# Turning the gated keys and queries in a recurrent attention plus FFN kernel: copies in destination order for the first chunk, DMA transposes for the later units

## The chip, the core and the metric

The kernel runs on one core of one Trainium2 chip. TensorE (PE in the profile; PEld is its weight load), VectorE (DVE), ScalarE (ACT), GpSimd (POOL) and SyncE (SP) each run their own instruction stream in order and meet through semaphores. Transfers are issued from SP's, ACT's or POOL's stream and run on 16 DMA engines. The metric is the time of one execution on the device, in microseconds; of several runs the median is taken.

## The reference

Inputs `q`, `k`, `v`, `f_logit` have the shape (4, 8, 768, 48): batch, heads, steps, head dimension. Per batch and head a 48 x 48 state is carried over 768 steps, and the result goes through a two-layer FFN:

```
f = 1 / (1 + exp(-f_logit))
for t in range(S):
    state = f[t][:, None] * state + outer(k[t], v[t])
    y[t] = q[t] @ state
x = y, heads side by side, as (B * S, 384)
out = leaky_relu(x @ w_in, 0.01) @ w_out        # 384 -> 2048 -> 384
```

## The kernel before

Steps are cut into six chunks of 128. One chunk of one batch, with all eight heads, is a *unit*: 24 units, numbered chunk by chunk, four batches to a chunk. Inside a unit the recurrence becomes matmuls. With L the running sum of -log f, keys are multiplied by exp(L) (`em_t`) and queries by exp(-L) (`a_t`); these scaled tiles `kh`, `qh` have the steps on the partitions and the eight heads, padded from 48 to 64, along the free dimension. They are then turned, so that head dimensions lie on the partitions, two heads to a block of 128: `kT`, `qT`. Scores are `kT` against `qT` (`score_pe`, 8 matmuls), masked to the upper triangle (`mask_dve`), multiplied with v, and the state's part is added (`mix_pe`). `state_pe`, `state_dve`, `state_pool` carry the state on. The result is copied (`y_out`), transposed (`x_pe`, `x_out`) and goes into the FFN, where two units form one row block of 256: `up` (6 matmuls of 256 columns per bank), `up_act` (leaky ReLU on ACT), `down` (8 matmuls of 384 columns, called twice per unit), `put` (copy on DVE and an output store issued on SP). The first row blocks use the narrower `up_one`, `down_cols` and `put_cols`.

Turning a unit (`turn_pe`, line 325) is eight PE transposes into one PSUM bank, then two DVE copies out of it (`turn_k`, `turn_q`, line 328).

The first chunk (units 0 to 3) is done four batches at once in a *quad* layout: partition 4t+b holds four neighbouring steps 4t to 4t+3 (index j) of batch b. It is computed in two halves of four heads (`hh`). `q_exp_act`, `q_ln_act` make the log gates, `q_gate_pe` their running sum, `q_decay_act` the two exponentials, `q_k_scale`, `q_q_scale` the scaled tiles, `q_turn_pe` their transposes. A transposed tile has in its free dimension the order j, t, b. `q_k_out`, `q_q_out` copy it out of PSUM into `kTq`, `qTq`, which are ordered b, t, j. Line 216 and its neighbours give that copy the order of the source: both sides are walked as j, t, b, so that neighbouring writes lie 256 bytes apart. The lines seen in the profile for these copies are those of the helper `move` (L138 on ACT, L140 on DVE), which also serves `cast_v`, `y_out`, `x_out` and `q_back_out`. `q_score_pe`, `q_mask`, `q_mask_pool`, `q_mix_pe` then do for the quad what the unit functions do later. `idle_pe` issues matmuls on zeros whose result nobody reads (L132).

The order of everything is written out by hand: 868 calls, one after the other, each with its PSUM bank numbers. Every engine runs its part of the list in that order. `load_part` calls (f, k, q, v of a unit; 192 KB each, on SP, in rings of six buffers) and the stores of `put` stand in the same list, so SP's stream is a fixed interleaving of loads and stores; a store waits on SP for DVE's copy, and what stands behind it waits too. At most eight transfers issued from SP and ACT are outstanding: each waits for the landing of the eighth before it.

The FFN weights are cast and loaded by POOL (`load_w_in`, `load_w_out`).

Of the kernel before, what the change touches and what calls it, by code (L numbers as in the profile page):

```python
# [9 lines left out]
FP32 = mybir.dt.float32  # L10
# [6 lines left out]
def kernel(  # L17
# [45 lines left out]
    fq = [const.tile([128, 4, 4, D], FP32, name=f"fq{i}", tag=f"fq{i}") for i in range(2)]  # L63
    kq = const.tile([128, H, 4, D], FP32, tag="kq")
    qq = [const.tile([128, 4, 4, D], FP32, name=f"qq{i}", tag=f"qq{i}") for i in range(2)]

    def load_quad(eng, t, src, b, lo, n):
        eng.dma_start(out=t[b::4, :, :, :].rearrange("p h j d -> p h (j d)"),
                      in_=src[b, lo:lo + n, 0:C, :].rearrange("h (t j) d -> t h (j d)", j=4))

    for hh in range(2):
        for b in (2, 3):
            load_quad(nc.scalar, fq[hh], f_logit, b, 4 * hh, 4)
    for hh in range(2):
        for b in (0, 1):
            load_quad(nc.sync, fq[hh], f_logit, b, 4 * hh, 4)
    for b in range(B):
        load_quad(nc.sync, kq, k, b, 0, H)
    for hh in range(2):
        for b in range(B):  # L80
            load_quad(nc.sync, qq[hh], q, b, 4 * hh, 4)

    nc.scalar.preload_act_table_set("natural_log_exp_and_others")
# [27 lines left out]
    qhs = [const.tile([128, H, 64], BF16, name=f"qh{i}", tag=f"qh{i}") for i in range(3)]  # L111
    khs = [const.tile([128, H, 64], BF16, name=f"kh{i}", tag=f"kh{i}") for i in range(4)]
# [12 lines left out]
    for t in lfs + khs + qhs:  # L125
        nc.vector.memset(t[:, :, D:64], 0.0)
    for t in state_b:
        nc.vector.memset(t, 0.0)
# [19 lines left out]
    turned = {name: ring(name, 3, [128, P2, 128], BF16) for name in ("kT", "qT")}  # L148
# [36 lines left out]
    def q_exp_act(hh):  # L185
        nc.scalar.activation(fq[hh], fq[hh], AF.Exp, scale=-1.0)

    def q_ln_act(hh):
        nc.scalar.activation(lfq[hh][:, :, :, 0:D], fq[hh].rearrange("p h j d -> p j h d"), AF.Ln, bias=1.0)
# [18 lines left out]
    def q_q_scale(eng, hh, a):  # L208
        q_scale_half(eng, qhq, qq[hh], aq, hh, a)
# [104 lines left out]
    def q_scale(u):  # L314
        r = raw[u]
        nc.gpsimd.tensor_mul(qhs[u % 3][:, :, 0:D], r["q"], a_ts[u % 3])  # L316
# [4 lines left out]
    def turn_pe(u, bk):  # L321
        tp = bank16(bk).rearrange("p (i a n) -> p i a n", i=2, a=P2)
        for i, src in enumerate((khs[u % 4], qhs[u % 3])):
            for p in range(P2):
                nc.tensor.transpose(tp[:, i, p, :], src[:, 2 * p:2 * p + 2, :], ident)  # L325

# [112 lines left out]
    idle_pe(31, 7)  # L439
# [8 lines left out]
    q_end_pe(2)  # L448
    q_gate_pe(1, 0, 3)
    q_decay_act(0, 0, emq, 1.0, 0)  # L450
    q_k_scale(V, 0, 1)
    q_end_act(2)
    q_k_scale(V, 0, 0)
    q_gate_pe(1, 1, 4)
    q_decay_act(0, 0, aq, -1.0, 0)
    q_decay_act(0, 1, aq, -1.0, 1)
    q_q_scale(V, 0, 0)
    q_turn_pe(khq, 0, 0, 5)
    q_turn_pe(khq, 0, 1, 5)
    q_decay_act(1, 1, emq, 1.0, 4)  # L460
    q_q_scale(G, 0, 1)
    q_turn_pe(qhq, 0, 0, 6)
    q_k_out(V, 0, 0, 5)
    idle_pe(4, 7)
    q_decay_act(1, 1, aq, -1.0, 4)
    q_decay_act(1, 0, emq, 1.0, 3)
    q_k_scale(G, 1, 1)
    q_k_out(V, 0, 1, 5)
    q_turn_pe(qhq, 0, 1, 6)
    idle_pe(7, 7)  # L470
    q_decay_act(1, 0, aq, -1.0, 3)
    q_k_scale(V, 1, 0)
    q_q_out(A, 0, 0, 6)
    q_q_scale(G, 1, 0)
    cast_v(V, 0)
    q_turn_pe(khq, 1, 0, 7)
    q_q_out(A, 0, 1, 6)
    q_turn_pe(khq, 1, 1, 7)
    q_q_scale(V, 1, 1)
    load_w_in(0)  # L480
    q_turn_pe(qhq, 1, 0, 2)
    q_k_out(V, 1, 0, 7)
    q_score_pe(0, 1, 0, 1)
    load_w_in(1)
    q_turn_pe(qhq, 1, 1, 2)
    q_wf_act(0, 1, 0, 0)
    q_k_out(V, 1, 1, 7)
    q_score_pe(0, 0, 4, 5)
    cast_v(G, 1)
    idle_pe(2, 6)  # L490
    q_q_out(A, 1, 0, 2)
    cast_v(G, 2)
    q_mask(0, 1, 1, 1)
    q_back_pe(3, 3)
    idle_pe(6, 7)
    q_mask_pool(0, 1, 0)
    q_q_out(A, 1, 1, 2)
    q_mask(0, 0, 1, 5)
    q_score_pe(1, 0, 6, 0)
    q_mask(0, 0, 0, 4)  # L500
    idle_pe(3, 7)
    load_w_in(2)
    q_mask(1, 0, 0, 6)
    q_score_pe(1, 1, 7, 1)
    load_w_in(3)
    idle_pe(7, 5)
    q_wf_act(1, 1, 1, 1)
    load_w_out(0)
    q_mask(1, 0, 1, 0)
    q_wf_act(1, 1, 0, 7)  # L510
    q_back_out(V, 3, 3)
    q_mix_pe(0, 2)
    q_mask_pool(1, 1, 1)
    q_mix_pe(1, 5)
    q_back_pe(0, 4)
    y_out(A, 0, 2)
    y_out(V, 1, 5)
    idle_pe(2, 7)
    q_back_out(A, 0, 4)
    x_pe(0, 6)  # L520
    x_pe(1, 1)
    q_mask_pool(1, 1, 0)
    q_back_pe(2, 0)
    x_out(A, 0, 6)
    x_out(V, 1, 1)
    state_pe(0, 3)
    q_back_out(V, 2, 0)
    up(0, 0, 7)
    q_state_dve(0)
    cast_v(G, 3)  # L530
    q_mix_pe(2, 2)
    up(0, 1, 5)
    up_act(0, 0, 7)
    y_out(V, 2, 2)
    q_state_pool(0)
    up(0, 5, 4)
    up_act(0, 1, 5)
    x_pe(2, 1)
    up(0, 4, 6)
    up_act(0, 5, 4)  # L540
    x_out(V, 2, 1)
    q_mix_pe(3, 0)
    load_part(4, "f", f_logit)
    state_pe(3, 3)
    up_act(0, 4, 6)
    up(0, 7, 7)
    y_out(V, 3, 0)
    q_state_dve(3)
    up(0, 6, 2)
    load_part(4, "k", k)  # L550
    up_act(0, 7, 7)
    x_pe(3, 5)
    q_state_pool(3)
    up(0, 2, 1)
    up_act(0, 6, 2)
    load_part(4, "q", q)
    x_out(A, 3, 5)
    state_pe(2, 4)
    q_back_pe(1, 6)
    q_state_dve(2)  # L560
    up(0, 3, 0)
    up_act(0, 2, 1)
    load_part(4, "v", v)
    up(1, 0, 3)
    q_back_out(V, 1, 6)
    q_state_pool(2)
    up_act(0, 3, 0)
    state_pe(1, 7)
    up(1, 7, 2)
    up_act(1, 0, 3)  # L570
    q_state_dve(1)
    up(1, 4, 5)
    up_act(1, 7, 2)
    q_state_pool(1)
    down_cols(0, 0, 1)
    up_act(1, 4, 5)
    gate_exp(4)
    up(1, 2, 4)
    gate_ln(4)
    put_cols(0, 0, 1)  # L580
    up(1, 1, 6)
    up_act(1, 2, 4)
    gate_pe(4, 0)
    up_act(1, 1, 6)
    up(1, 6, 3)
    decay_em(4, 0)
    load_w_out(1)
    up(1, 5, 7)
    decay_a(4, 0)
    down_cols(1, 0, 2)  # L590
    k_scale(4)
    up_act(1, 5, 7)
    up_act(1, 6, 3)
    load_part(5, "f", f_logit)
    q_scale(4)
    up(1, 3, 5)
    put_cols(1, 0, 2)
    cast_v(G, 4)
    turn_pe(4, 1)
    load_part(5, "k", k)  # L600
    up_act(1, 3, 5)
    state_pe(4, 4)
    turn_k(4, 1)
    down_cols(3, 0, 6)
    load_part(5, "q", q)
    state_dve(4)
    turn_q(4, 1)
    down_cols(2, 0, 0)
    load_part(5, "v", v)
    put_cols(3, 0, 6)  # L610
    load_part(6, "f", f_logit)
    score_pe(4, 7, 3)
    put_cols(2, 0, 0)
    down_cols(3, 1, 2)
    mask_dve(4, 1, 3)
    load_part(6, "k", k)
    mask_dve(4, 0, 7)
    gate_exp(5)
    down_cols(0, 1, 5)
    load_part(6, "q", q)  # L620
    put_cols(3, 1, 2)
    gate_ln(5)
    load_part(6, "v", v)
    mix_pe(4, 4)
    put_cols(0, 1, 5)
    gate_pe(5, 1)
    state_pool(4)
    y_out(A, 4, 4)
    down_cols(2, 1, 6)
    load_part(7, "f", f_logit)  # L630
    decay_em(5, 1)
    decay_a(5, 1)
    k_scale(5)
    load_part(7, "k", k)
    x_pe(4, 0)
    down_cols(1, 1, 3)
    put_cols(2, 1, 6)
    x_out(V, 4, 0)
    gate_exp(6)
    q_scale(5)  # L640
    load_part(7, "q", q)
    gate_ln(6)
    up_one(4, 3, 7)
    cast_v(G, 5)
    put_cols(1, 1, 3)
    load_part(7, "v", v)
    turn_pe(5, 2)
    up_one_act(4, 3, 7)
    up_one(4, 1, 5)
    turn_k(5, 2)  # L650
    load_part(8, "f", f_logit)
    turn_q(5, 2)
    up_one(4, 0, 4)
    up_one_act(4, 1, 5)
    cast_v(G, 6)
    gate_pe(6, 1)
    load_part(8, "k", k)
    up_one_act(4, 0, 4)
    score_pe(5, 6, 0)
    up_one(4, 2, 3)  # L660
    decay_em(6, 1)
    mask_dve(5, 0, 6)
    load_part(8, "q", q)
    gate_exp(7)
    k_scale(6)
    down(4, 0, 7)
    mask_dve(5, 1, 0)
    gate_ln(7)
    load_part(8, "v", v)
    up_one_act(4, 2, 3)  # L670
    mix_pe(5, 2)
    decay_a(6, 1)
    state_pe(6, 5)
    gate_pe(7, 4)
    load_part(9, "f", f_logit)
    state_dve(6)
    down(4, 1, 7)
    y_out(A, 5, 2)
    q_scale(6)
    decay_em(7, 4)  # L680
    load_part(9, "k", k)
    decay_a(7, 4)
    cast_v(G, 7)
    x_pe(5, 6)
    turn_pe(6, 0)
    put(4, 7)
    k_scale(7)
    gate_exp(8)
    state_pe(5, 3)
    load_part(9, "q", q)  # L690
    x_out(V, 5, 6)
    gate_ln(8)
    turn_k(6, 0)
    up_one(5, 3, 1)
    q_scale(7)
    state_dve(5)
    load_part(9, "v", v)
    up_one(5, 1, 2)
    up_one_act(5, 3, 1)
    turn_q(6, 0)  # L700
# [636 lines left out]
```

## Time and profile before

| | |
|---|---|
| median of three runs | 203.26 us (203.01 to 205.38) |
| profiled execution, own time | 203.25 us |
| its span in the profile | 201.5 us |
| PE busy | 186.6 us (93%) |
| DVE, ACT, POOL busy | 96.5, 120.6, 82.1 us |
| first `up` matmul (L402) starts | 31.22 us |
| turning transposes (L325) | 160 matmuls |
| copies of turned units (L328) | 40, mean 423 and 416 ns |
| quad copies (L138, L140, 128x512 bf16 of kTq, qTq) | 8, mean 2532 ns on DVE, 2622 ns on ACT (the second of a pair overlaps the first's start) |
| a load of 192 KB, issue to landing | 3.9 us (median) |

The span is from the first to the last instruction; the execution's own time adds what lies around it, 1.75 us here. Busy times of PE are from modelled ends: its matmuls overlap, so that a group's pitch (time from one start to the next) is what it costs in a full stream, and this is shorter than the mean duration shown. In the timeline, a line gives start, duration, engine, source line, operation, output and inputs, count, and in brackets the idle time ahead of it with what ended it.

### The profile page before, as it was taken

The page shows a single profiled execution, that of the slowest core. Times are in us where ns is not written, and L with a number is a line of the kernel's source. Part 1 is how long each engine was busy: PE and PEld are TensorE (multiplying, and loading weights), DVE is VectorE, ACT ScalarE, POOL GpSimd, SP SyncE. Part 2 cuts the span into 40 slices and gives each one's busy share as a digit, 9 for nine tenths or more (in the row PEclk, how much of TensorE's full clock was granted, in tenths as well). Part 3 has the DMA queues.
Part 4 walks back from the last instruction along what each step waited for, and adds up shares of the span by engine and source line. Part 5 has one row for each costly group of instructions (what it writes and reads, how often), then busy time and mean ns, then how long its engine had stood idle before and what let it go on. Part 6 is the DMA issues. An engine that isn't in the chain of part 4 may idle for free.

```text
span 201.5 us, 5284 instructions
## 1 busy us (share of the span) xinstructions
PE 186.6 (93%) x2094; PEld 146.6 (73%) x2094; DVE 96.5 (48%) x215; ACT 120.6 (60%) x237; POOL 82.1 (41%) x144
## 2 busy tenths in 40 slices
PE   4993599999999979999999999999999999999991
PEld 3782368999997748787778767877878877776660
DVE  6069955405445836954656456333555460111221
ACT  2678935883456768768778666766656734343200
POOL 4046742442444768795467581671632000000000
PEclk9998559999999999999999999999999999999998
DMA  4878999099988999999999899722100011111121
GB/s 130 239 179 129 221 195 164 0 89 226 199 195 183 233 190 235 185 217 188 219 192 235 174 229 204 160 47 74 42 0 3 0 42 39 39 39 42 41 108 50
DMA packets 100537, 27.08 MB, mean 134 GB/s; under 512 B 92320, under 2 KB 100512, under 8 KB 100512
## 3 DMA queue, kind: packets, MB, share of 16 engines
q1 hardware_dynamic: 94208, 23.21, 52.5%
q0 software_dynamic: 5728, 3.15, 11.8%
q10 hardware_dynamic: 576, 0.39, 0.8%
q8 instruction: 16, 0.26, 0.5%
q14 instruction: 9, 0.07, 0.1%
HBM read 25.17 MB, written 4.72 MB: 148 GB/s over the span
## 4 chain that ended last, share of the span: by engine, by line
PE 78%; DVE 6%; DMA 6%; POOL 3%; issue 3%; SPq 2%; ACT 1%; POOLq 0%; DVEq 0%; ACTq 0%
PE ps L402 29%; PE ps L416 23%; PE ps L132 5%; DVE kTq L140 4%; PE ps L325 4%; PE ps L427 3%; PE ps L341 3%; DMA v_raw<-in_v_dram 2%; DMA k_raw<-in_k_dram 2%; DMA f_raw<-in_f_logit_dram 2%; PE ps L385 2%; PE ps L354 2%; PE ps L351 1%; PE ps L362 1%; PE ps L194 1%
## 5 line engine op out<-in xcount | busy, mean ns | idle before, releaser
L411 ACT ACTIVATE gT<-ps 128x512 bf16<-128x512 f32 x88 | 52.1, 597 | 33.8 <-PE ps L402 31.7
L402 PE MATMUL ps<-xT,w_in_b 128*128 128x256 bf16 x528 | 67.8, 273 | 0.2 <-DVE xT L140 0.2
L416 PE MATMUL ps<-w_out_b,gT 128*128 128x384 bf16 x320 | 56.9, 326 | 0.0
L402 PEld LDWEIGHTS <-w_in_b 128*128 128x128 bf16 x528 | 49.1, 98 | 8.0 <-issue 0.3
L416 PEld LDWEIGHTS <-gT 128*128 128x128 bf16 x320 | 30.3, 98 | 17.2
L344 DVE TENSOR_TENSOR wm<-ps,ut 128x512 bf16<-128x512 f32 x40 | 25.9, 686 | 11.1 <-PE ps L341 9.4
L422 DVE COPY osb<-ps 128x384 f32<-128x384 f32 x20 | 11.1, 557 | 37.1 <-PE ps L416 37.1
L312 POOL TENSOR_TENSOR kh<-k_raw,em_t 128x384 bf16<-128x384 f32 x20 | 18.1, 913 | 12.1 <-ACT em_t L304 5.2
L281 POOL CAST sb<-sf 64x192 bf16<-64x192 f32 x40 | 13.6, 341 | 22.8 <-PE ps L351 14.8
L316 POOL TENSOR_TENSOR qh<-q_raw,a_t 128x384 bf16<-128x384 f32 x20 | 18.1, 911 | 4.7 <-ACT a_end L309 1.4
L140 POOL CAST v_b<-v_raw 128x384 bf16<-128x384 f32 x23 | 11.8, 512 | 13.9 <-DMA v_raw<-in_v_dram 10.2
L328 DVE COPY kT<-ps 128x512 bf16<-128x512 bf16 x20 | 8.5, 423 | 16.3 <-PE ps L325 12.7
L288 ACT ACTIVATE f_raw<-f_raw 128x384 f32<-128x384 f32 x20 | 10.5, 526 | 9.4 <-DMA f_raw<-in_f_logit_dram 9.4
L138 ACT CAST xn<-ps 128x384 bf16<-128x384 f32 x21 | 10.0, 480 | 9.6 <-PE ps L354 8.6
L132 PE MATMUL ps<-fill 128*128 128x256 bf16 x65 | 13.4, 373 | 1.1 <-DVE ind L124 1.1
L140 DVE COPY xT<-ps 128x384 bf16<-128x384 bf16 x22 | 7.7, 352 | 8.7 <-PE ps L385 4.7
L427 PE MATMUL ps<-w_out_b,gT 128*128 128x192 bf16 x128 | 11.5, 246 | 0.0
L132 PEld LDWEIGHTS <-fill 128*128 128x128 bf16 x65 | 8.0, 129 | 4.4 <-issue 1.9
L304 ACT ACTIVATE em_t<-ps 128x384 bf16<-128x384 f32 x20 | 9.9, 495 | 2.1 <-PE ps L300 1.4
L291 ACT ACTIVATE lf<-f_raw 128x384 bf16<-128x384 f32 x20 | 10.5, 524 | 0.5
L427 PEld LDWEIGHTS <-gT 128*128 128x128 bf16 x128 | 10.5, 98 | 0.1
L307 ACT ACTIVATE a_t<-ps 128x384 bf16<-128x384 f32 x20 | 9.8, 495 | 0.0
(92 smaller groups left out, 240.5 us busy)
## 6 DMA issues: line engine op xcount, KB each, us to landing
v_raw<-in_v_dram SPq DMA_DIRECT2D x24, 192.0 KB, 3.9
f_raw<-in_f_logit_dram SPq DMA_DIRECT2D x20, 192.0 KB, 3.9
k_raw<-in_k_dram SPq DMA_DIRECT2D x20, 192.0 KB, 4.0
q_raw<-in_q_dram SPq DMA_DIRECT2D x20, 192.0 KB, 3.9
out_dram<-osb SPq DMA_DIRECT2D x20, 192.0 KB, 1.9
w_in_b<-in_moe_w_in_dram POOLq DMA_DIRECT2D x4, 384.0 KB, 7.2
w_out_b<-in_moe_w_out_dram POOLq DMA_DIRECT2D x2, 768.0 KB, 11.3
kq<-in_k_dram SPq DMA_DIRECT2D x4, 192.0 KB, 3.8
```

What stands on the lines that cost most here:

```text
L132: nc.tensor.matmul(bank(bk)[:, 0:256], fill[:, 0:128], fill[:, 0:256], start=True, stop=True)
L140: eng.tensor_copy(out=out, in_=in_)
L281: nc.gpsimd.tensor_copy(out=state_b[b][r, :, e * D:(e + 1) * D], in_=state_f[b][r])
L288: nc.scalar.activation(raw[u]["f"], raw[u]["f"], AF.Exp, scale=-1.0)
L312: nc.gpsimd.tensor_mul(khs[u % 4][:, :, 0:D], raw[u]["k"], em_ts[u % 3])
L316: nc.gpsimd.tensor_mul(qhs[u % 3][:, :, 0:D], r["q"], a_ts[u % 3])
L344: nc.vector.tensor_mul(wms[e][u % 3], bank(bk).rearrange("p (i n) -> p i n", i=P2), ut[:, None, :].to_broadcast([128, P2, 128]))
L402: nc.tensor.matmul(bank(bk)[:, i * 256:(i + 1) * 256], w_in_b[:, kk, ff * 128:(ff + 1) * 128], xTs[m % 3][:, kk].rearrange("p a n -> p (a ...
L411: nc.scalar.activation(gTs[m % GBUFS][:, 2 * g:2 * g + 2].rearrange("p f a n -> p (f a n)"), bank(bk), AF.Prelu, alpha=0.01)
L416: nc.tensor.matmul(bank(bk)[:, 0:KD], gTs[u // 2 % GBUFS][:, ff, u % 2, :], w_out_b[:, ff, :], start=(ff == 0), stop=(ff == NF - 1))
L422: nc.vector.tensor_copy(out=osb, in_=bank(bk)[:, 0:KD])
L427: nc.tensor.matmul(bank(bk)[:, 0:CH], gTs[u // 2 % GBUFS][:, ff, u % 2, :], w_out_b[:, ff, half * CH:(half + 1) * CH], start=(ff == 0), st ...
```

## The change

Three things are different, and the call list is written anew around them.

- **First loads.** f and q of the quad are one tile each, with all heads, in place of two halves: four loads each, not eight. Two of the four k loads go from SP to ACT, behind the table load.
- **Quad copies in destination order.** `q_turn_out` walks both sides as b, t, j. The writes are then contiguous, and the reads from PSUM are 256 bytes apart. The eight copies are also distributed anew: six on ACT, two on DVE (before, four and four).
- **Units 10 to 23** are turned by `turn_dma`, one DMA transpose on SP from the scaled tiles to the turned ones (128 x 1024 bf16, 256 KB). `turn_pe`, `turn_k`, `turn_q` remain for units 4 to 9. For this `kh` and `qh` of a unit become the halves of one tile `kqh`, in a ring of four (`qh` had three), and `kT`, `qT` the halves of one tile `kqT`, in a ring of three.

In the new list the fill matmuls ahead of the first gate go from 31 to 40, most of the first chunk's mixing stands ahead of the first `up`, and unit 5's four loads stand ahead of the first output store (before, behind it). From unit 10 on, loads stand behind each `turn_dma` in SP's stream. The counts of all FFN calls are as before.

```diff
-    fq = [const.tile([128, 4, 4, D], FP32, name=f"fq{i}", tag=f"fq{i}") for i in range(2)]
+    fq = const.tile([128, H, 4, D], FP32, tag="fq")
...
-    for hh in range(2):
-        for b in (2, 3):
-            load_quad(nc.scalar, fq[hh], f_logit, b, 4 * hh, 4)
...
+    for b in (2, 3):
+        load_quad(nc.scalar, fq, f_logit, b)
+    nc.scalar.preload_act_table_set("natural_log_exp_and_others")
+    for b in (2, 3):
+        load_quad(nc.scalar, kq, k, b)
+    for t, src in ((fq, f_logit), (kq, k)):
+        for b in (0, 1):
+            load_quad(nc.sync, t, src, b)
+    for b in range(B):
+        load_quad(nc.sync, qq, q, b)
...
+    kqs = ring("kqh", 4, [128, 2, H, 64], BF16)
+    khs, qhs = [t[:, 0] for t in kqs], [t[:, 1] for t in kqs]
...
+    kqTs = ring("kqT", 3, [128, 2, P2, 128], BF16)
+    turned = {"kT": [t[:, 0] for t in kqTs], "qT": [t[:, 1] for t in kqTs]}
...
     def q_turn_out(dst, hh, bk, pp):
-        tp = bank16(bk).rearrange("p (a j t b) -> p a j t b", a=2, j=4, b=4)
-        o = dst[hh].rearrange("p a b (t j) -> p a j t b", j=4)
-        return dict(out=o[:, pp], in_=tp[:, pp])
+        tp = bank16(bk).rearrange("p (a j t b) -> p a b t j", a=2, j=4, b=4)
+        return dict(out=dst[hh][:, pp].rearrange("p b (t j) -> p b t j", j=4), in_=tp[:, pp])
...
+    def turn_dma(u):
+        nc.sync.dma_start_transpose(out=kqTs[u % 3].rearrange("p i a n -> p (i a) n"),
+                                    in_=kqs[u % 4].rearrange("p i h d -> p (i h d)"))
...
-    idle_pe(31, 7)
+    idle_pe(40, 7)
...
-    turn_pe(15, 1)
...
-    turn_k(15, 1)
...
-    turn_q(15, 1)
-    score_pe(15, 5, 3)
...
+    q_scale(15)
...
+    turn_dma(15)
+    score_pe(14, 2, 6)
...
+    score_pe(15, 5, 3)
```

More of the change, by code (lines that the diff above doesn't have):

```diff
@@ L734 @@
[L734 to L741 removed]
+    load_part(7, "v", v)
+    score_pe(5, 5, 0)
+    put_cols(1, 1, 1)
+    down_cols(3, 1, 3)
+    mask_dve(5, 1, 0)
+    load_part(8, "f", f_logit)
+    mask_dve(5, 0, 5)
+    gate_pe(6, 4)
+    x_pe(4, 2)
+    put_cols(3, 1, 3)
+    load_part(8, "k", k)
+    mix_pe(5, 6)
+    decay_em(6, 4)
+    x_out(V, 4, 2)
+    state_pe(5, 7)
+    decay_a(6, 4)
@@ new lines @@
+    gate_pe(8, 5)
+    state_pool(6)
+    turn_pe(7, 6)
+    load_part(10, "k", k)
+    decay_em(8, 5)
+    down(5, 0, 1)
+    turn_k(7, 6)
+    decay_a(8, 5)
+    turn_q(7, 6)
+    k_scale(8)
+    y_out(A, 6, 7)
+    score_pe(7, 0, 3)
+    load_part(10, "q", q)
+    x_pe(6, 4)
+    cast_v(G, 8)
+    up_one(5, 3, 5)
+    mask_dve(7, 1, 3)
+    q_scale(8)
+    gate_exp(9)
+    state_pe(8, 6)
+    mask_dve(7, 0, 0)
+    up_one(4, 3, 7)
+    up_one_act(5, 3, 5)
+    load_part(10, "v", v)
+    state_dve(8)
@@ new lines @@
+    up(6, 4, 5)
+    load_part(19, "f", f_logit)
+    score_pe(16, 7, 4)
+    up_act(6, 4, 5)
+    mix_pe(15, 0)
+    mask_dve(16, 0, 7)
+    gate_pe(17, 1)
+    state_pool(15)
+    y_out(A, 15, 0)
+    up(6, 0, 6)
+    mask_dve(16, 1, 4)
+    decay_em(17, 1)
+    x_pe(15, 3)
+    up(6, 2, 5)
+    decay_a(17, 1)
+    load_part(19, "k", k)
+    x_out(V, 15, 3)
+    k_scale(17)
+    mix_pe(16, 7)
+    up_act(6, 0, 6)
+    down(11, 1, 2)
+    load_part(19, "q", q)
+    q_scale(17)
+    y_out(A, 16, 7)
@@ new lines @@
+    gate_exp(20)
+    up(7, 6, 0)
+    state_dve(19)
+    q_scale(18)
+    load_part(21, "k", k)
+    gate_ln(20)
+    up(7, 3, 4)
+    y_out(A, 17, 3)
+    turn_dma(18)
+    gate_pe(20, 7)
+    load_part(21, "q", q)
+    up_act(7, 6, 0)
+    state_pe(18, 6)
+    x_pe(17, 1)
+    down(12, 1, 5)
+    state_dve(18)
+    decay_em(20, 7)
+    load_part(21, "v", v)
+    up_act(7, 3, 4)
+    k_scale(20)
+    x_out(V, 17, 1)
+    up(8, 5, 2)
+    put(12, 5)
+    score_pe(19, 3, 0)
+    up_act(8, 5, 2)
```

1441 lines of the change are left out of this document (661 added, 780 removed).

## The prediction

> **What bounds the kernel now.** I first read the 40 slices of the page (each is 5.04 us).
>
> ```profile
> PE   4993599999999979999999999999999999999991
> PEclk9998559999999999999999999999999999999998
> DMA  4878999099988999999999899722100011111121
> GB/s 130 239 179 129 221 195 164 0 89 226 199 195 183 233 190 235 185 217 188 219 192 235 174 229 204 160 47 74 42 0 3 0 42 39 39 39 42 41 108 50
> ```
>
> TensorE (PE) is short of work and at half clock around slices 4 to 6, then full to the end. The transfers are at capacity to slice 25 except for a hole in slices 8 and 9 (0 and 89 GB/s). So there are two stages, with the border at the first wide FFN matmul. The timeline of the first 32 us shows what delays that one:
>
> ```profile
> 13.25 4.70 DVE L140 COPY kTq<-ps 128x512 bf16<-128x512 bf16 x2 [0.47 <-PE ps L215]
> ...
> 17.58 0.75 DVE L203 TENSOR_TENSOR khq<-kq,emq 128x384 bf16<-128x384 f32 x1
> ...
> 19.30 4.68 DVE L140 COPY kTq<-ps 128x512 bf16<-128x512 bf16 x2
> ...
> 31.22 0.82 PE L402 MATMUL ps<-xT,w_in_b 128*128 128x256 bf16 x6 [0.22 <-DVE xT L140]
> ```
>
> One copy of a turned tile takes 2.35 us here, and two pairs stand one after the other on VectorE (DVE), with the scaling of the second half between them. From 31.2 us on, this is all that PE waits for (waits of PE, 31 to 200 us):
>
> ```profile
> PE ps L297 <- ACT lf L291: 1.2, 1, 1.2
> PE ps L325 <- POOL qh L316: 0.7, 2, 0.4
> PE ps L402 <- DVE xT L140: 0.2, 1, 0.2
> ```
>
> The chain that ended last is then PE throughout from 76 us, and it gives each group's price at full clock, free of the modelled overlap:
>
> ```profile
> 86.05 1.30 PE ps L416 x8
> 87.35 0.45 PE ps L325 x8
> ...
> 93.28 1.31 PE ps L402 x12
> 94.60 0.33 PE ps L341 x8
> ```
>
> So 0.109 us for a 256-column matmul of `up`, 0.163 for `down`, 0.057 for a transpose, 0.041 for a score, likewise 0.083 for L427 (1.32 by 16). Multiplying out the calls after the first `up`, with the small groups from the same view, gives 162 us of PE work between 31.2 and the last matmul's end at 197.2: 166 us, so about 4 us are lost there. **PE's instruction count is the bound after 31 us; before that it is a chain through copies.** Lastly the SP queue in order of time:
>
> ```profile
> 22.07 2.43 SPq L158 DMA_DIRECT2D v_raw<-in_v_dram  x1
> 41.87 0.36 SPq L434 DMA_DIRECT2D out_dram<-osh  x1
> 42.28 0.99 SPq L158 DMA_DIRECT2D f_raw<-in_f_logit_dram  x1
> ...
> 127.60 0.43 SPq L158 DMA_DIRECT2D v_raw<-in_v_dram  x1
> ```
>
> SP sits 17.4 us behind the first output store: that is the hole. From 42.3 to 127.6 it issues 74 loads and 17 stores, so 0.94 us a transfer (1.15 if stores are free). I take **1.1 us as a load's slot.**
>
> **The change, part by part.**
>
> *First loads.* Sixteen half loads of f, q become eight whole ones. f now comes in one piece: before, ScalarE (ACT) started on the first half at 5.31 and on the second at 7.27, after 0.24 us of waiting for it. The bytes are the same, so all of f should land between 5.3 and 7.2; I take 6.3. Four table passes of 0.84 us, of which the first two matter, bring the first gate's input to 8.2. But the fill ahead of it grows from 31 to 40 matmuls, and 31 took 6.39 us, so 40 take 8.2 and PE is free at 11.2, against 9.4. (At the 0.11 us that later fills show it would be 10.4.) This costs +1.8 us at most. All of q is there at 12.2 to 12.6 before, as late as it is needed.
>
> *Destination-order copies.* The same 512 elements are written in a row, and read from PSUM 256 bytes apart. Nothing in the trace reads PSUM like this. The ends: 0.42 us (DVE) and 0.59 us (ACT), the dense 128x512 copies at L140 and L138, and 2.35 us, the scattered write. I take 0.59, since what sets the slow row apart from the dense one is its writes, and these become dense. The order also moves four k copies: ACT now does six, DVE two. Following the queues: gates end near 12.6, ACT's eight exponentials (0.5 each) and the small one run to about 17, its copies then at 0.6 each, so the first half's scores can start near 19.8 (19.17 before) and the second's near 20.6 (25.54 before). From there masks (DVE 0.72; POOL 1.15 each, four in a row, the longer queue), mixing, `y_out` 0.5, `x_pe`, `x_out` take some 7 us, as POOL has to finish before mixing. **First `up` at 27.5, against 31.2: -3.7 us.**
>
> *Transposes.* Units 10 to 23 lose 8 transposes each on PE: 14 x 8 x 0.057 = 6.4 us, and 28 DVE copies of 0.42 us = 11.8 us, worth nothing by themselves (DVE is 48% busy). The new order also has some 1.1 us of mixing and turning of the first chunk ahead of the first `up`, where PE waits anyway. **PE work after it: 154.7 instead of 162.2, -7.5 us.**
>
> *What they become.* 14 transfers of 256 KB on SP. The trace has no such transfer. From below: 0.87 us, 256 KB at 303 GB/s, the fastest microsecond in the trace (6 to 7 us). From above: 3.8 us, at the 11.3 us that `w_out`'s 768 KB takes to land. I take a load's slot, 1.1 us: 1024 pieces of 256 bytes against a load's 1024 of 192. The room: in the new order, PE work between the gates of unit 10 and unit 23 is 72 us for 13 units, 5.54 us a unit; four loads and a store of 0.94 to 1.1 us with one transpose make 5.6. It just fits, with a lead of 2 to 3 us, which comes from unit 5's loads now being ahead of the first store (4 x 1.1 us) and the earlier first `up`.
>
> *The added wait.* Each transpose waits on SP for POOL's two scalings (0.91 us each) and for the last reader of its buffer on PE. Loads of units five or six ahead are queued behind it, whose data are wanted 20 us later, so this head-of-line wait is covered unless it recurs at several us. What is not covered is the landing: between the transpose and its `score_pe` the order has only 3.8 to 6.5 us of PE work (mean 5.1). A load lands in 3.9 us, and POOL's 0.9 may still be running: at 4.8 us the shortfalls of the 14 sum to 3 us, at 4.5 to 1.3, at 5.5 to 8.4. **I take +3.0 us.**
>
> **Sum:** the profiled execution took 203.25 us (span 201.5), the median of the three runs is 203.26, so one stands for the other. 203.25 - 3.7 - 7.5 + 3.0 = **195.0 us**, own range 190 to 200.
>
> **The rivals.**
>
> *A. Strided PSUM reads are as slow as scattered writes.* Then six ACT copies cost 1.76 us more each, five of them ahead of the first scores: first `up` near 37, +6 instead of -3.7. With PE later, the loads lead more and the stalls shrink to 1.5: 203.25 + 6 - 7.5 + 1.5 = 203. For it: element-by-element jumps are only moved from one side to the other. Against: DVE's f32 copies out of PSUM take 557 ns for 384 elements (L422) and 357 for 192 (L433), 1.04 ns an element of 4 bytes; at one access per 2-byte element 512 would cost about as much each, 0.5 us and the start. [...] Chance 0.13.
>
> *B. A transpose occupies the transfer engines far longer than a load (the slower side).* Place: units 10 to 23, where PE would wait for its gates' input, since the loads fall behind by the excess each unit. Price: 13 units x (t - 1.1) less the 2.4 us lead. It takes back the whole 11.2 us at t = 2.1 us, and from 2.5 us the kernel is over 2% slower; at 2.6 it is 203.25 - 11.2 + 17.1 = 209; at the upper row's 3.8, 225. For it: DMA is at 0.95 to 1.04 busy in these slices. Against: the number of pieces. [...] Chance 0.20.
>
> *C. All fits.* Landings within 4 us and fill at the faster rate: first `up` at 26.9, no new stalls, 203.25 - 4.3 - 7.5 = 191.4. Chance 0.12.
>
> **How the numbers follow.** Forecast 0.55, A 0.13, B 0.20, C 0.12. Predicted 195.0. Low 188, below C by the share of the 4 us of present stalls that another order may lose or save; high 208, which takes in A and the mild end of B: about 0.8 inside. A measurement tells 2% (4.1 us) from no change: faster than 199.2 holds C and nearly all of the forecast, 0.66; slower than 207.3 holds B less its mild end, 0.19; 0.15 between.
>
> **What would show it.** Copies at L138/L139 under 0.8 us, first `up` at 26 to 29 us; 112 fewer transposes, and DVE busy down by about 20 us (28 copies, and four scattered ones gone or short); transposes landing in 4 to 5 us; PE waiting in all 3 to 5 us for them at the scores; ACT's wait for f_raw not above the 9.4 us of now. Wrong would be: copies over 2 us (A), or f_raw and v_raw waits of 20 us and PE slices below 9 from 70 to 140 us (B).

## The result, and the profile after

The changed kernel takes 193.05 us (median; 191.31 to 194.47), the kernel before 203.13 beside it (201.73 to 205.38): a ratio of 0.950, 95% interval [0.939, 0.960]. The forecast was 195.0. The profiled execution took 192.82 us, with a span of 190.8. Ratios here and below leave out single executions that were disturbed and took over 1.5% longer than the fastest, so that a ratio can differ a little from the quotient of two medians; the profiled executions of e5 and e7 are such ones, so that what only their profiles show is not certain. The median of the kernel before came out between 203.1 and 205.4 us on different occasions, so runs are compared by their ratios to the kernel before of the same occasion (which takes it that the other kernels drift alike; this was not tried), or profile against profile.

The 40 slices of the page after (each 4.77 us):

```profile
PE   4998959999999999999989979999899999999991
PEclk9999999999999999999999999999999999999999
DMA  5999999987799998989989999969993840001112
GB/s 158 321 200 159 175 180 168 198 129 177 172 213 203 177 235 183 207 169 223 206 149 176 234 209 169 226 132 230 208 216 74 215 100 0 3 0 41 63 61 84
```

Three things differ from before. PE is well filled from slice 2 on but for slice 6, just ahead of the first wide `up`, and the half clock of slices 4 to 6 is gone. The hole behind the first store has shrunk to a dip (129 GB/s in slice 9, where 0 and 89 stood in slices 8 and 9). And the transfers stay full up to slice 30, some 143 us, instead of slice 25, some 126.

The timeline of the first 29 us, with the lines of ACT, DVE and PE that answer to the slow copies and to the first `up`:

```profile
14.67 0.58 ACT L137 COPY kTq<-ps 128x512 bf16<-128x512 bf16 x1 [0.39 <-PE ps L215]
...
17.73 0.69 DVE L139 COPY qTq<-ps 128x512 bf16<-128x512 bf16 x1 [0.72 <-PE ps L215]
...
22.39 0.43 DVE L139 COPY kqh<-ps 128x512 bf16<-128x512 bf16 x1
23.27 0.59 ACT L137 COPY kqh<-ps 128x512 bf16<-128x512 bf16 x1 [1.56 <-PE ps L264]
...
28.07 1.48 PE L405 MATMUL ps<-xT,w_in_b 128*128 128x256 bf16 x12 [1.55 <-DMA w_in_b<-in_moe_w_in_dram]
```

A quad copy takes 0.58 to 0.62 us on ACT and 0.68 to 0.69 on DVE, where it took 2.35. The `kqh` lines are dense copies of the same size in the same stretch: reading PSUM 256 bytes apart costs ACT nothing, and DVE 0.26 us. The first `up` starts at 28.07 instead of 31.22, and what it waits for is no longer a copy: it is the weights.

The waits of PE (us in all, times, longest), of which L344 lies behind the first `up` and the two others ahead of it:

```profile
PE ps L344 <- DMA kqT<-kqh: 2.4, 3, 1.0
...
PE ps L405 <- DMA w_in_b<-in_moe_w_in_dram: 1.5, 1, 1.5
PE ps L388 <- DVE xn L139: 0.7, 1, 0.7
```

The chain that ended last, in the kernel before and then after: its pieces that are transfers (start, duration, what).

```profile
56.03 3.75 DMA f_raw<-in_f_logit_dram
...
64.01 3.79 DMA v_raw<-in_v_dram
...
70.02 3.79 DMA k_raw<-in_k_dram
```

```profile
16.85 11.18 DMA w_in_b<-in_moe_w_in_dram
28.07 1.48 PE ps L405 x12
...
92.64 5.35 DMA kqT<-kqh
...
108.92 4.03 DMA kqT<-kqh
...
128.44 5.68 DMA kqT<-kqh
```

Three late loads stood in the old chain. None stands in the new one; a quarter of w_in and three transposes have taken their places.

And the transposes, by their tile; the second line is the time from issue to landing:

```profile
L327 SPq DMA_TRANSPOSE kqT<-kqh x14: 1237/1538/3502, 73.5 to 154.3; - x14
...
DMA to landing us min/median/max: 3.1/3.7/5.7
```

They land as fast as a load (3.6 to 4.0 us here), but hold SP's queue for 1.24 us at least, where the shortest loads of a unit hold it for 0.4 us (0.37 to 0.43).

The difference of the two profiles splits at the first `up` (the second column is the end of the last `down`, taken from the timeline as start plus duration). All runs of the study stand in this table; the last column is what PE needed from its first wide matmul to its last.

| kernel | ratio to before [95%] | first `up` | last matmul ends | between |
|---|---|---|---|---|
| before | 1 | 31.22 | 197.16 | 165.9 |
| after | 0.950 [0.939, 0.960] | 28.07 | 186.60 | 158.5 |
| e1, after with copies in source order | 0.981 [0.974, 0.988] | 35.31 | 194.51 | 159.2 |
| e3, after turned on PE | 0.979 [0.971, 0.987] | 28.21 | 193.11 | 164.9 |
| e10, new order with neither edit | 1.017 [1.010, 1.023] | 37.20 | 202.09 | 164.9 |
| e2, before with copies in destination order | 0.988 [0.982, 0.993] | 23.33 | 196.11 | 172.8 |
| e7, e2 with unit 5's loads ahead | 0.975 [0.967, 0.984] | 25.22 | 196.33 | 171.1 |
| e8, e7 with weights earlier | 0.977 [0.970, 0.985] | 22.83 | 196.07 | 173.2 |
| e11, e8 without 16 loads | 0.970 [0.961, 0.979] | 25.11 | 194.54 | 169.4 |
| e5, after with each transpose twice | 1.003 [0.997, 1.010] | 28.24 | 202.43 | 174.2 |
| e6, after without transposes | 0.923 [0.916, 0.931] | 27.83 | 183.71 | 155.9 |
| e4, after with w_in in the order of use | 0.941 [0.934, 0.947] | 25.33 | 185.57 | 160.2 |
| e9, e4 with w_out earlier | 0.940 [0.935, 0.945] | 26.87 | 185.61 | 158.7 |

So 10.6 us between the last matmuls of before and after: 3.15 came ahead of the first `up`, 7.4 behind it.

### The profile page after: what moved, and what is told of

Read it like the earlier page. It is cut to its first block, busy times and chain, and to the rows that moved or that the text cites. A ratio compares the mean times of both kernels' runs of the same rounds, so it can differ in the third digit from the quotient of the medians.

```text
span 190.8 us, 5057 instructions
## 1 busy us (share of the span) xinstructions
PE 178.2 (93%) x2006; PEld 140.4 (74%) x2006; DVE 80.8 (42%) x185; ACT 113.1 (59%) x239; POOL 81.0 (42%) x142
## 3 DMA queue, kind: packets, MB, share of 16 engines
q0 software_dynamic: 5728, 3.15, 12.3%
## 4 chain that ended last, share of the span: by engine, by line
PE 79%; DMA 14%; POOL 4%; ACT 1%; DVE 0%; issue 0%; POOLq 0%; DVEq 0%
PE ps L405 27%; PE ps L419 24%; DMA kqT<-kqh 8%; DMA w_in_b<-in_moe_w_in_dram 6%; PE ps L430 6%; PE ps L131 4%; PE ps L344 3%; PE ps L398 3%; PE ps L357 2%; PE ps L354 2%; PE ps L388 2%; PE ps L296 2%; PE ps L324 1%; PE ps L365 1%; POOL w_in_b L167 1%; PE ps L194 1%
## 5 line engine op out<-in xcount | busy, mean ns | idle before, releaser
L311 POOL TENSOR_TENSOR kqh<-k_raw,em_t 128x384 bf16<-128x384 f32 x20 | 18.2, 911 | 35.9 <-ACT em_t L303 27.1
L425 DVE COPY osb<-ps 128x384 f32<-128x384 f32 x20 | 11.2, 558 | 36.9 <-PE ps L419 36.7
L315 POOL TENSOR_TENSOR kqh<-q_raw,a_t 128x384 bf16<-128x384 f32 x20 | 18.2, 911 | 0.6 <-ACT a_end L308 0.5
L139 DVE COPY xT<-ps 128x384 bf16<-128x384 bf16 x24 | 8.5, 356 | 20.2 <-PE ps L388 20.1
L131 PEld LDWEIGHTS <-fill 128*128 128x128 bf16 x89 | 9.2, 108 | 3.2 <-issue 1.3
L373 DVE TENSOR_TENSOR sf<-sf,ps 64x192 f32<-64x192 f32 x16 | 5.5, 343 | 12.7 <-ACT gT L414 6.4
L139 POOL CAST v_b<-v_raw 128x384 bf16<-128x384 f32 x21 | 10.5, 503 | 0.4
L287 ACT ACTIVATE f_raw<-f_raw 128x384 f32<-128x384 f32 x20 | 10.6, 529 | 0.0
L344 PE MATMUL ps<-kqT 64*128 64x128 bf16 x160 | 7.9, 219 | 2.4 <-DMA kqT<-kqh 2.4
```

Source lines behind the costliest of these rows:

```text
L131: nc.tensor.matmul(bank(bk)[:, 0:256], fill[:, 0:128], fill[:, 0:256], start=True, stop=True)
L139: eng.tensor_copy(out=out, in_=in_)
L311: nc.gpsimd.tensor_mul(khs[u % 4][:, :, 0:D], raw[u]["k"], em_ts[u % 3])
L315: nc.gpsimd.tensor_mul(qhs[u % 4][:, :, 0:D], r["q"], a_ts[u % 3])
L344: nc.tensor.matmul(bank(bk)[:, p * 128:(p + 1) * 128], kT[r, p, :], qT[r, p, :], start=True, stop=True)
L425: nc.vector.tensor_copy(out=osb, in_=bank(bk)[:, 0:KD])
```

## The experiments

### The order of the copies, in the new kernel and in the old one (e1, e2)

In the new kernel, `q_turn_out` alone is put back:

```diff
-        tp = bank16(bk).rearrange("p (a j t b) -> p a b t j", a=2, j=4, b=4)
-        return dict(out=dst[hh][:, pp].rearrange("p b (t j) -> p b t j", j=4), in_=tp[:, pp])
+        tp = bank16(bk).rearrange("p (a j t b) -> p a j t b", a=2, j=4, b=4)
+        o = dst[hh].rearrange("p a b (t j) -> p a j t b", j=4)
+        return dict(out=o[:, pp], in_=tp[:, pp])
```

> The changed kernel, with only the eight quad copies walked in source order again. My theory: what made a copy take 2.35 us was its scattered writes, and the first up waits for the copies' chain. Then the copies are back at 2.3 to 2.4 us (0.54 to 0.58 us on ACT and 0.69 on DVE in the changed kernel); ACT has six of them, five ahead of the first half's last score, so the first scores start 8 to 9 us later than 18.5 us and the first up at 35 to 36 us in place of 28.1; after that PE's work is the same. Time about 200.5 us. Rival: the first up is held by the arrival of w_in and by the rest of the first chunk, so that most of the copies' time lies beside it; then the first up moves by 3 us at most, time 196 or less.

Measured: ratio 0.981, profiled execution 200.78 us against 192.82. ACT's timeline in this run, and the wait of PE that ends on it:

```profile
18.43 5.04 ACT L137 COPY kTq<-ps 128x512 bf16<-128x512 bf16 x2
...
22.96 5.04 ACT L137 COPY qTq<-ps 128x512 bf16<-128x512 bf16 x2
```

```profile
PE ps L233 <- ACT qTq L137: 7.8, 2, 6.6
```

The copies are slow again (5.04 us a pair), PE stands 6.6 us at the scores, and the first `up` comes at 35.31. From there to the end the run takes 159.2 us, as the changed kernel does (158.5). The write order is thus worth 7.2 us ahead of the first `up`, all of which reaches the end (the last matmul ends 7.9 us later). It also brings the half clock back: in the two microseconds behind that wait (27 to 29 us) the granted clock is 0.50.

The same edit alone in the kernel before, in the other direction:

> The kernel before, with only the eight quad copies walked in destination order. My theory: two pairs in a chain on DVE shrink from 4.7 us to about 1.4 us each; first up at 25 to 27 us in place of 31.2; the rest of the kernel is bound by PE's work and follows, time 197.5 to 199. Rival: what follows is paced by the loads, whose hole behind the first store stays in this order, so PE only waits later for f and v; then PE's waits after the first up grow from 2 us to 4 or more and the time is 200 to 202.

Measured: 0.988, so 2.5 us, where the same edit is worth 6 to 8 in the new order (e1 against after, and e10 against e3, below). The copies are fast (0.59 to 0.64 us on ACT, 0.68 to 0.69 on DVE) and the first `up` comes at 23.33 us, 7.9 earlier than before and earlier than expected. Then 6.9 of the 7.9 us are lost again behind it (172.8 against 165.9). PE's waits:

```profile
PE ps L401 <- DMA w_in_b<-in_moe_w_in_dram: 3.1, 2, 1.9
...
PE ps L426 <- DMA w_out_b<-in_moe_w_out_dram: 1.4, 1, 1.4
PE ps L296 <- ACT lf L290: 1.4, 1, 1.4
...
PE ps L324 <- POOL qh L315: 0.6, 1, 0.6
```

Here are three stretches of the same run: busy time of PE, PEld, DVE, ACT and POOL with instruction counts, the granted clock, the DMA share and GB/s.

```profile
70.00:73.00 3.00, 1.14 (x19) 0.71 (x15) 1.09 (x3) 2.14 (x5) 2.57 (x6) 0.99 0.99 193
73.00:77.00 4.00, 3.94 (x31) 2.80 (x32) 1.08 (x3) 2.01 (x7) 3.93 (x5) 0.58 1.01 223
77.00:80.00 3.00, 3.00 (x43) 2.70 (x40) 2.67 (x7) 2.26 (x5) 0.70 (x2) 1.00 1.02 204
```

A stop of under 2 us at 70.6, behind a late k load (the chain has it landing at 71.3), is followed by 3.4 us at half clock (over the 4 us to 77 the mean of the granted clock is 0.58; at 0.50, as e7 shows it below, for 3.4 us and 1.00 for the rest it comes to that), in which PE counts as busy all the time. The waits list shows the stop and not this second price. My expectation of a gain near 5 us fell; the rival, that transfers take the gain back, held: PE's waits behind the first `up` are 6.7 us here against 2.1 before, 4.5 of them for the weights. Which transfers is the question of e7, e8 and e11.

### Turning on PE, and neither edit: the square (e3, e10)

In the changed kernel each `turn_dma` of units 10 to 23 goes out, and the three calls that it replaced go into a free bank some 2 us ahead of the score:

```diff
-    turn_dma(10)
...
+    turn_pe(10, 6)
+    turn_k(10, 6)
+    turn_q(10, 6)
```

> The changed kernel in its own order, but units 10 to 23 are turned by eight PE transposes and two DVE copies again, in a PSUM bank that is free there, with about 2 us of PE work up to the scores. My theory: PE is the bound, so 112 transposes of 0.057 us come back, 6.4 us, and the 2.4 us that PE waits for the DMA transposes go: 193 + 4 = 197 us, first up unchanged at about 28 us. Rival: the gain after the first up came from the new order of the calls, not from the PE work taken out; then PE's time after the first up grows by less than 2 us, time under 195.

Measured: 0.979, profiled 199.28 us. First `up` at 28.21, as in the changed kernel, and 164.9 us behind it instead of 158.5: +6.4 us. That is as much as 112 transposes at 0.057 us, but it is a net figure: the 2.4 us of waits for `kqT` are gone, which is why I had expected 2.4 us less, and others have come (1.7 us, 1.5 of them at `x_out`'s result), so some 0.7 us more than the transposes' price came back, and where is not shown. The rival, that the new order alone explains the gain, fell. The fourth corner is this kernel with e1's diff on top, so the new order with neither edit:

> The new order of calls with neither edit: quad copies in source order and units 10 to 23 turned on PE. It completes the square of the two edits in the new order (both 193.0, without the destination order 200.9, without the transposes 200.0). Theory (both edits shorten PE's own time line, one before the first up and one after it, so that they add): 193.0 + 7.9 + 7.0 = 207.9 us, first up near 35.3; the new order by itself is then 4 us slower than the old one. Rival (the later start of PE hides part of what the turning on PE costs, or the new order is worth something by itself): 203 or less.

Measured: 207.7 us, 1.017 [1.010, 1.023]. The two edits add, as expected, to within the intervals: 0.950 + 0.031 + 0.029 = 1.010.

| ratio to before | turned on PE | DMA transposes from unit 10 on |
|---|---|---|
| copies in source order | 1.017 | 0.981 |
| copies in destination order | 0.979 | 0.950 |

The new order by itself is therefore no gain, it costs 1.7% (the joined first loads, which no run tries by themselves, are part of it): with six slow copies in one row on ACT its first `up` comes at 37.20, 6.0 us later than before (in this execution the fill alone took 1.4 us longer than in e1, see the last section), and it wins 1.0 back behind it (164.9 against 165.9). What it is good for shows only with the fast copies: e2 against e3, 0.988 against 0.979 with intervals that overlap; in the profiles the first `up` comes 4.9 us later, and still the end 3.0 us earlier.

### What a transpose costs (e5, e6)

Each transpose once more, into tiles that nobody reads:

```diff
+        nc.sync.dma_start_transpose(out=kqDs[u % 3].rearrange("p i a n -> p (i a) n"),
+                                    in_=kqs[u % 4].rearrange("p i h d -> p (i h d)"))
```

> The changed kernel with every DMA transpose of units 10 to 23 issued twice, the second one into tiles that nobody reads: 14 more transfers of 256 KB, nothing else. Theory (a transpose takes the transfer engines some 1.45 us, and the loads are only 2 to 5 us ahead of their gates): the ten of units 10 to 19, which stand ahead of unit 23's loads, set these back by 10 x 1.45 = 14.5 us less 2.5 us of lead, so about 193 + 12 = 205 us, with PE waiting at the gates (lf) and ACT for f_raw. By the 1.1 us that the forecast used: 201.5. Rival (a transpose holds an engine's queue but hardly any transfer room, so that the landing alone counts): 193 to 195. A transpose that occupies far longer than seen so far, 4 us and more, would show as 230 and more.

Measured: 1.003 [0.997, 1.010], which is 0.0536 above the changed kernel and so 10.9 us (expected 12; the rival that a transpose takes hardly any room, 0 to 2). SP's queue shows where it goes, with unit 23's first load in this run and then in the changed kernel:

```profile
151.81 0.76 SPq L159 DMA_DIRECT2D f_raw<-in_f_logit_dram  x1
```

```profile
136.44 1.09 SPq L158 DMA_DIRECT2D f_raw<-in_f_logit_dram  x1
```

Ten more transposes stand ahead of it, and it is issued 15.4 us later: 1.5 us for one transpose in a full stream of transfers. By the ratio it is 10.9 us and the 2.5 of lead, so 1.3. That agrees with the shares of the DMA engines in the changed kernel, where three transposes and three stores (0.55 us each, since the share is 0.11 from 170 to 175 us, where one store is all that moves) between 146 and 153 us add up to 5.87 us, so 1.4 each. And here is the busiest DMA queue of the changed kernel, against that of e6, which has no transposes (packets, MB, the time of the packets as a share of the span of 190.8 and then 187.8 us):

```profile
q1 hardware_dynamic: 108352, 26.49, 68.4%
```

```profile
q1 hardware_dynamic: 93568, 22.81, 56.7%
```

The 24 us between them are 1.7 us for each of 14, somewhat too much, since such shares read up to 1.15 in a full microsecond (147 to 148 us in the changed kernel). So **about 1.5 us for one transpose**, between 1.3 and 1.7. Only the place was not as expected: PE waits at the scores, not at the gates.

```profile
PE ps L347 <- DMA kqT<-kqh: 11.4, 6, 2.8
```

The landing itself is hardly longer than in the changed kernel (median 3.9 us against 3.7). Why the lateness gathers at this link was not tried.

The opposite, no transpose at all:

```diff
-    turn_dma(10)
...
-    turn_dma(23)
```

> The changed kernel without the 14 DMA transposes: the turning of units 10 to 23 is left out, their scores read what the tiles still hold. Theory (all that the transposes cost PE is the 2.4 us of waits at three scores): 193.0 - 2.4 = 190.6 us, PE waits for kqT gone, w_in's 1.5 still there. Rival (they also cost by taking room from the loads and by holding SP's queue, which shows as small waits spread over the other groups): 188 or less. Rival (the waits for kqT only stand in place of others, so that nothing comes off): 193.

Measured: 0.923 [0.916, 0.931]; the profiled execution took 189.83 us, 3.0 less than the changed kernel's. PE's waits behind the first `up` are gone, and what is left is ahead of it:

```profile
PE ps L405 <- DMA w_in_b<-in_moe_w_in_dram: 1.5, 1, 1.5
PE ps L131 <- DVE ind L121: 1.1, 1, 1.1
PE ps L388 <- DVE xn L139: 0.7, 1, 0.7
```

Behind the first `up` it takes 155.9 us, 2.6 less, against the 2.4 us of waits for `kqT`; so profile against profile the theory holds. By ratios it does not: the theory's 190.6 us is 0.938 of the kernel before, above the interval, the rival's 188 is 0.926, and the step from the changed kernel is 3 to 8 us. So the rival of spread-out small costs is not excluded; which of the two comparisons is right was not tried.

### Where the gain of e2 went (e7, e8, e11)

The old order with fast copies, and unit 5's loads moved ahead of the first store, so that SP does not sit on them:

```diff
+    load_part(5, "f", f_logit)
+    load_part(5, "k", k)
+    load_part(5, "q", q)
+    load_part(5, "v", v)
     put_cols(0, 0, 1)
```

> The kernel before with copies in destination order (202.2 us) and the four loads of unit 5 moved ahead of the first output store in SP's stream. In that run PE stood still at 70.6 to 72.6 us behind a late k load and then had half its clock until 76.5. Theory (the loads held behind the first store make that stall): it goes with its clock loss, some 4 us, while the waits for w_in (3.1) and w_out (1.4) stay: 198 us. Rival (the transfer engines are at capacity there anyway, so that the loads now take room from the weights): 201 to 203, with w_out's wait grown.

Measured: 0.975 [0.967, 0.984], profiled 202.42 us. In this profile the stop at 70 us and its half clock are still there:

```profile
70.00:72.00 2.00, 0.66 (x12) 0.48 (x11) 1.09 (x3) 0.97 (x3) 1.33 (x4) 1.00 0.66 127
72.00:74.00 2.00, 1.28 (x15) 0.98 (x15) 0.00 (x0) 1.84 (x7) 1.92 (x3) 0.76 1.02 202
74.00:76.00 2.00, 2.00 (x11) 1.44 (x10) 0.76 (x2) 0.60 (x1) 2.00 (x4) 0.50 1.05 233
```

And the wait for w_out has grown from 1.4 to 2.5 us, as the rival had it, while the one for w_in has shrunk from 3.1 to 0.7, behind a first `up` that comes 1.9 us later. So in this profile the hole behind the first store does not make the stall, and my theory fell there. By time it stays open: the ratio lies between the theory's (198 us, 0.969 beside the kernel before of e2) and the rival's (from 0.984), and its interval takes in the one and touches the other. Next the weights, earlier on POOL:

```diff
     cast_v(G, 2)
+    load_w_in(2)
+    load_w_in(3)
+    load_w_out(0)
...
     q_state_pool(3)
+    load_w_out(1)
```

> As the run with unit 5's loads ahead of the first store, and on POOL the last two quarters of w_in and the first half of w_out issued ahead of the masks, the second half of w_out two state copies earlier. Theory (what was left of the 7.9 us of the earlier first up was lost to late weights): the waits for w_in go from 3.1 to under 1.5 and those for w_out to 0, so 195 to 196 us, which is the time before less the 7.9 us. Rival (bytes, not their order, set when the weights are there): no better than the run without it, about 198.

Measured: 0.977 [0.970, 0.985], no better than e7, as the rival had it (though both, at 201 us, lie above the 198 that I had given them). The wait for w_out is gone, that for w_in is 2.9 us, and now ACT waits for its gate input all along: 12.3 us in nine places, 9.4 in the kernel before, 0.0 in the changed one. Putting the 20 gates in a row explains it. From unit 4's to unit 23's first gate pass (`gate_exp`, from ACT's timeline):

| | unit 4 | unit 23 | per unit | last f load issued |
|---|---|---|---|---|
| before | 40.59 | 130.66 | 4.74 us | 125.5 |
| e8 | 35.64 | 129.58 | 4.94 us | 124.5 |
| after | 33.05 | 143.11 | 5.79 us | 136.4 |
| e11 (below) | 38.19 | 128.05 | 4.73 us | 118.4 |

e8 starts its units 5 us earlier than before and finishes them 1 us earlier. Four loads and a store of 192 KB a unit at 4.74 us are 207 GB/s, which is what the transfers brought in e8 between 60 and 110 us, at a DMA share of 0.91 to 1.00 (189 to 210 GB/s). So the old order seems to ask for units as fast as they can come at most, and could not use an earlier start. To test this, 16 loads are left out of e8:

```diff
-        nc.sync.dma_start(out=t, in_=src[b, :, c * C:(c + 1) * C, :].rearrange("h t d -> t h d"))
+        if name != "v" or u < 8:
+            nc.sync.dma_start(out=t, in_=src[b, :, c * C:(c + 1) * C, :].rearrange("h t d -> t h d"))
```

> As the run of the old order with copies in destination order, unit 5's loads ahead and weights early (201.1 us, first up at 22.8), but without the v loads of units 8 to 23: 16 loads of 192 KB are left out, and those units read the v of unit u - 6 that still lies in the buffer. No other work is changed. Theory (the old order asks for a unit every 4.7 to 5 us, which is what the transfer engines can bring at most, so that an earlier first up only finds the loads late): ACT's wait for f_raw goes from 12.3 us to under 3, PE's short waits at 66 to 78 and 110 to 126 us go, some 4 us, and the last gate comes well before 129.6: 196 to 197.5 us. Rival (the order itself, by what waits for POOL, ACT and the banks, holds PE up there): 200 us or more.

Who waited for `f_raw` (us in all, times), in e8 and then in this run:

```profile
  ACT f_raw L287: 12.3, 9
```

```profile
  ACT f_raw L288: 1.3, 1
```

One wait of 1.3 us is left of nine. PE, which stood 3.0 us in all between 110 and 130 us in e8, is idle for 0.3 us in all from 40 to 160 us, and the time behind the first `up` falls from 173.2 to 169.4 us. With a fifth fewer bytes a unit the gates run at 4.73 us, so this is the order's own pace, and the 4.94 of e8 is what the transfers made of it. But the time came to 0.970 [0.961, 0.979], which overlaps e8's, and the last matmul ends only 1.5 us earlier: in the profiled execution PE had waited 2.0 us for a scaled q ahead of the first `up` (25.11 instead of 22.83). A later start alone gives the loads some lead, and e7, with all loads and its first `up` at 25.22, takes 171.1 us behind it. So the loads are shown as the cause of the waits in the middle of the run, and they are worth between 1.7 and 3.8 us there; what is left of the loss of e2 lies at the weights (3.4 us in e11) and, 1.6 us, at a late gate.

### The order of the weights in the changed kernel (e4, e9)

The first `up` of the new order is `up(0, 7, 7)`, which reads the last quarter of w_in. e4 loads the quarters as 3, 1, 2, 0:

```diff
-    load_w_in(0)
+    load_w_in(3)
...
-    load_w_in(3)
+    load_w_in(0)
```

> The changed kernel with the four quarters of w_in loaded in the order 3, 1, 2, 0 in place of 0, 1, 2, 3: the first up in the list reads quarter 3, which is the last to be loaded, and PE waited 1.55 us for it. My theory: that wait goes, first up at 26.5 to 27 us, time 1.0 to 1.5 us lower, about 191.7. Rival: the transfers are at capacity there, all quarters land late, and the wait only moves to the next up that reads another quarter; then no change, 193.

Measured: 0.941 [0.934, 0.947], profiled 191.72. First `up` at 25.33, 2.7 us earlier; 1.7 of these are given back at a new wait, the one for w_out:

```profile
PE ps L344 <- DMA kqT<-kqh: 1.8, 3, 0.9
PE ps L430 <- DMA w_out_b<-in_moe_w_out_dram: 1.7, 1, 1.7
```

e9 also issues the second half of w_out right behind the first:

```diff
     load_w_out(0)
+    load_w_out(1)
...
-    load_w_out(1)
```

> The run with w_in's quarters in the order of use (3, 1, 2, 0), and the second half of w_out issued on POOL right behind the first half, not behind the state copies (30.1 us there, landing at 42.5). Theory (its 12.4 us of landing began too late, so that it is the issue that has to move): the 1.7 us wait for w_out goes, PE's next wait is for a transpose, and the time comes to about 190.5 us, 0.935 of the kernel before. Rival (the transfer engines are at capacity up to 40 us, so that w_out takes room from the loads of units 4 and 5 and the wait moves to their gates): 192 to 193, 0.943 or more, with waits for lf instead.

Measured: 0.940 [0.935, 0.945], between the theory's 0.935 and the rival's 0.943 and the same as e4; the waits for lf that the rival named did not come. The wait for w_out is halved (0.9 us), but the halves now take 17.6 and 23.5 us to land (17.3 and 12.4 in e4), and the first `up` in this execution comes at 26.87 (0.9 of the 1.5 us by a longer fill). Up to 40 us the transfers are full (in e4 the DMA share is 0.98 to 1.41 from 5 to 40 us), and here an earlier issue of the second half only made its landing longer. Of the kernels that leave no work out, e4 and e9 are the fastest, by about 1% against the changed one, with intervals that overlap its own.

## Why the prediction was right, and where it was off

**First `up`: 27.5 forecast, 28.07 measured.** The copies came out as taken (0.59 us; 0.58 to 0.62 on ACT, 0.69 on DVE; three k copies went to ACT and one q copy to DVE, not four k copies), all of f was there at 6.2 (6.3 forecast), the scores of the two halves at 18.50 and 20.04 (19.8 and 20.6 forecast), and x was ready at 26.5, a microsecond earlier than forecast. Two sizes were off and cancel in part, so that being within 0.6 us is in part luck. The fill: the forecast had 40 matmuls end at 11.2; they ended at 9.45, hardly later than 31 before (9.39). And the weights: I listed every engine ahead of the first `up` and not the last quarter of w_in, which costs 1.55 us; in e4, which takes it away, the first `up` comes 2.7 us earlier (0.5 of it from a shorter fill; some 0.6 are not accounted for).

**PE work behind it: -7.5 us forecast.** The transposes' 6.4 us agree with e3, whose +6.4 us is a net of transposes and waits. The other 1.1 (mixing moved ahead) was not tried alone; e10 needs 1.0 us less than before behind its first `up`, 0.4 of it because it waits less there.

**Stalls: +3.0 us forecast, about 0 measured, which is the term that made 195.0 out of 192.** The landings themselves were sized well: PE waits 2.4 us for them, and without them the time behind the first `up` falls by 2.6 (e6). What I left out is that the new order also ends the stalls of the old one: the 2.1 us for gates, queries and xT are gone. A unit now has 5.79 us and not 4.74 to be brought in, the three loads left the chain, and ACT, which in the kernel before waited for `f_raw` (us in all, times) as below, does not wait for it at all; nor does it in e3 and e10, which have the new order without the transposes.

```profile
  ACT f_raw L288: 9.4, 8
```

I had used the new pace (5.54 us) only to ask if the transposes fit.

**The room.** A transpose takes about 1.5 us in a full stream, not 1.1. The forecast's 5.6 us a unit was too small by its own terms: five transfers at 0.94 and 1.1 for the transpose are 5.8, at 1.1 for each 6.6. With 1.5 it would be 6.2 against the 5.79 that a unit has, and the loads would fall back by 0.4 us a unit. They do not: by issue and landing in the trace, f lands 2.2 us ahead of its gate at unit 10, 3.0 ahead at unit 23, and between 1.6 and 4.6 in the units between. So the 0.94 a transfer, which counts SP's own waits too, was probably too much. "Just fits" came out right, with the lead of 2 to 3 us that was forecast, though by two errors that cancel; e5 shows that there is no room for a second transpose.

**Rival A fell**, and e1 shows that its price was near: with slow copies the first `up` comes at 35.3 (37 given) and the profiled execution takes 200.78 us (203 given). For the copies' PSUM reads here the loss is 0.26 us in 0.69 on DVE and none on ACT; the scattered SBUF writes took 2.35 us on either in the kernel before.

**Rival B fell.** Its break-even was 2.1 us a transpose; about 1.5 was measured, and all eight blocks of one land in 3.7 us. But e5 also shows where B would have begun: doubling this cost takes back all of the gain (1.003 of the kernel before).

**Signs named in advance.** As named: copies under 0.8 us, first `up` between 26 and 29, 112 transposes fewer, ACT's wait for f_raw 0.0 (not above 9.4). Smaller than named: DVE busy 80.8 us instead of 96.5 (-15.7, forecast -20; its copies of turned tiles are 20 us less by their rows, but the new list also gives DVE other copies and scalings), transposes landing at 3.7 us (4 to 5 given), and PE waiting 2.4 us for them (3 to 5 given).

## What to carry to other kernels

Before pricing an earlier start, work out how fast the order of calls asks for its inputs (here 4.74 us for 960 KB of loads and stores a unit) and set it against what the transfers bring (189 to 210 GB/s in e8, so 4.7 to 5.2 us for these 960 KB): the same edit was worth 6 to 8 us in an order that leaves room and 2.5 us in one whose loads and weights were already about as fast as the transfers bring them. When work moves off an engine onto transfers, count its full transfer time (about 1.5 us here) against the unit's pace and its landing (3.7 us) against the work between issue and use, and count also the stalls that the changed pace ends. A stop of PE can cost twice, once as the wait and once at half clock (in e2 1.9 us idle and then 3.4 us at half clock), and only the first is in the list of waits.

## What the runs showed of the hardware that was not expected

- **The fill's rate doubled at no fixed point.** The fill ahead of the first gate begins at 3.0 us in the kernel before, in the changed one and in e1 to e10. 31 matmuls took 5.65 to 6.39 us, 40 took 5.82 to 7.36. At the low rate one takes 0.21 us (31 in 6.39), at the high rate 0.11, as in later fills (7 in 0.93 us, 8 in 1.04, in the changed kernel). In the profile's half microseconds, which count every matmul that runs in them and so many of them twice, this shows as 3 to 5 at first and 7 later; the step comes near 5.5 us in e3, at 7.0 in the changed kernel and at 9.0 in e10, and in the profiled execution of the kernel before all 31 ran at the low rate. The granted clock reads 1.00 throughout, so the profile's clock row does not show it. So the step came some 2.5 to 6 us after the start of the matmuls, in the kernel before not within 6.39; what sets it is not shown. For the forecast it meant that the fill's length could not be known to better than a microsecond.
- **A scattered 2-byte write cost DVE and ACT the same**, 2.35 us for 512 a partition in the kernel before (4.6 ns each), while a copy that reads the same elements from PSUM with a stride and writes them in a row takes 0.58 to 0.62 (ACT) and 0.69 (DVE).
- **A DMA transpose of 128 x 1024 bf16** holds its issuing queue for 1.24 us or more, occupies the transfer engines for about 1.5 us (1.3 to 1.7 by four ways of counting), and lands 3.1 to 5.7 us after issue (median 3.7).
